# Two heads' maxima in the two halves of TensorE's rows, and a dense result loaded into the key buffer

## The chip, the cores and the metric

The kernel runs on one core of one Trainium2 chip. The metric is the device time of one execution in microseconds (us). Lower is better. Engines are named as in the profile: PE is TensorE, PEld its weight loads, DVE VectorE, ACT ScalarE, POOL GpSimd, SP SyncE, whose queue (SPq) issues all the DMAs of this kernel.

## The reference

The input `x` has 2048 rows of 512 numbers. Two branches are computed from it and mixed by a gate, one number per row:

```python
g = sigmoid((x * gate_w).sum(-1))
a = attention(x, wqkv) @ wo      # 32 heads of 16; a query sees itself and the 255 keys before it
b = gelu(x @ w1 + b1) @ w2 + b2  # 1792 hidden units, tanh form of GELU
out = g * a + (1 - g) * b
```

All of it is float32. In attention, `scores = q @ k * 16**-0.5`, masked to the sliding window, softmax over the keys, times `v`.

## The kernel before, in words

**Precision.** TensorE multiplies in a rounded format (`fp32r`). To keep float32 accuracy an operand is split into a high part and the rest, and a dense product is three matmuls: high x high, high x low, low x high (`mm3`, lines 89 to 92). For attention the same three terms are stacked along the contraction: a head's 16 numbers take 32 rows with high and low interleaved, and 16 rows more for the third term.

**The stacks.** `qs` and `ks` (lines 168 and 169) hold the stacked queries and keys of four heads at a time: two pairs `pr`, and in each pair two heads `s`. Rows 0 to 31 are the first head's high and low parts, rows 32 to 63 the second head's, rows 64 to 79 and 80 to 95 their third terms. Rows 96 to 103 of `qs` take the negated maxima of the rows, and `ks` has ones there at the head's own columns (`own`, `clear_k`). In `ks` each head's keys stand in columns of their own, blocks of 64 alternating between the heads, and the other head's rows are zero in them, so that a product over all rows gives one head's scores. `load_k` and `att_load` (lines 348 to 373) fill them by DMA from the stores SK and SQ, one chunk of 512 columns at a time.

**Attention** runs in 8 groups of four heads, each with 16 blocks of 128 queries: 128 units. For a unit:

- `att_max` (line 385): for each of four heads one matmul of the 128 queries with up to 384 keys into a PSUM buffer `sm` (three of them), and then on VectorE a reduction with the mask that gives the row's maximum (L399). `att_rows` negates and transposes four blocks' maxima, and GpSimd puts them into rows 96 to 103 of `qs`.
- `att_exp` (line 425): eight units later, four matmuls of keys with queries (L435, all 128 rows, so the maxima are subtracted in the product) into buffers `st`, ScalarE's exponential, and GpSimd's masks.
- `att_pv` (line 456): every fourth unit, the products with the values, in tiles of 64 rows by 32 columns (L476), into one buffer `st` and one `sm`. The result goes to memory (ND), is normalised in `att_norm`, and is stored as OT.

**The dense branch** is a generator (`dense`, line 726): the projections for q, k and v, then eight turns of `mlp` (four stretches of 512 rows, each with two halves of the hidden units; `gelu` is spread over ACT and DVE), then `final`, which multiplies the attention result with `wo` and mixes. A turn of the first half stores its sum in YA, a turn of the second half adds it and stores YB. `load_y` (line 676) loads YB into weight buffers `w`: the first stretch in the last turn, the others in `final`. `scale_y` multiplies with 1 - g in place, and L716 adds it to g times the product.

**The order** is written out by hand. The main loop (line 755) goes through the units; for each of four steps it issues one maximum (`i ^ XOR`), one score, and lets the generator run until 574 ns of dense matmuls are issued (`fill`, a quarter of STEP). What the other engines do is put into a list with a due time (`after`); `tick` advances a clock by an assumed cost of each matmul and issues what is due; `need` forces what must be there. So the assumed costs and delays (GELU, LAND, YLAND) set the order of instructions on ACT, DVE, POOL and SP, and not their time.

Of the kernel before, what the change touches and what calls it, by code (L numbers as in the profile page):

```python
# [9 lines left out]
F32 = mybir.dt.float32  # L10
# [8 lines left out]
T = 512  # L19
# [13 lines left out]
def gated_mix(ctx: ExitStack, tc: tile.TileContext, x, wqkv, wo, w1, b1, w2, b2, gate_w, out):  # L33
# [11 lines left out]
    def f32(ap):  # L45
        return ap.bitcast(F32)
# [3 lines left out]


    SQ = [dr.tile([H, 16, 2, T], F32, name=f"SQ{t}") for t in range(NT)]
    SK = dr.tile([H, 16, 2, S], F32, name="SK")
    SV = [dr.tile([T, H, 17], F32, name=f"SV{t}") for t in range(NT)]
    XT = [dr.tile([NC, 128, 2, T], F32, name=f"XT{t}") for t in range(NT)]
# [22 lines left out]
    for k in (0, 1):  # L78
        nc.gpsimd.affine_select(out=own[96:104], in_=own[96:104], pattern=[[-2, 4]], compare_op=ALU.not_equal,
                                fill=1.0, base=-k, channel_multiplier=1)  # L80
    nms = cp.tile([128, RB, 32], F32R, name="nm")
    nc.gpsimd.memset(f32(nms), 0.0)
    vbuf = cp.tile([128, 2, NB * 68 + 16], F32, name="vbuf")
# [76 lines left out]
    def load_now(key):  # L160
        load_raw(key)
        after(LAND, split, key, nc.vector)

# [182 lines left out]
    def load_k(g_, c, prs):  # L348


        need(("qk", c, NC + g_ // 2))
        for pr in range(prs.start, prs.stop):
            for s in range(2):
                src = SK[4 * g_ + 2 * pr + s]
                for r, n, part in ((32 * s, 32, src.rearrange("d u c -> (d u) c")), (64 + 16 * s, 16, src[:, 0])):
                    v = f32(ks[r:r + n, pr])
                    k0, m = (c * T, NB) if s == 0 else (c * T - 64, NB) if c else (64, NB - 1)
                    to = v[:, 2 * k0 + 64:2 * k0 + 64 + 256 * m] if s else v[:, 2 * k0:2 * k0 + 256 * m]
                    to = to.rearrange("r (n x) -> r n x", x=256)
                    to = to[:, :, 0:128] if s else to[:, :, 64:192]  # L360
                    nc.sync.dma_start(to, part[:, k0:k0 + 128 * m].rearrange("r (n x) -> r n x", x=128))
                    if s and c == 0:
                        nc.sync.dma_start(v[:, 0:64], part[:, 0:64])
                    if s and c == NT - 1:
                        nc.sync.dma_start(v[:, 2 * S - 64:2 * S], part[:, S - 64:S])

    def att_load(g_, c, q_only=False):
        need(("qk", c, g_ // 2))
        if not q_only:
            load_k(g_, c, slice(0, 2))  # L370
        src, to = SQ[c][4 * g_:4 * g_ + 4], f32(qs[:, :, c * T:(c + 1) * T])
        nc.sync.dma_start(to[0:64], src.rearrange("(a s) d u c -> (s d u) a c", a=2))
        nc.sync.dma_start(to[64:96], src[:, :, 1].rearrange("(a s) d c -> (s d) a c", a=2))

    def att_load_v(g_, c):
        need(*[("v", c, b) for b in range(NB)])
# [8 lines left out]
    def att_max(g_, b, i):  # L385

        if b % RB == 0 and (g_, b // RB) not in Ms:
            Ms[g_, b // RB] = sb.tile([128, RB, 4], F32, tag="M", bufs=2, name=f"M{g_}_{b}")
        M = Ms[g_, b // RB]
        k0 = max(b - 2, 0) * 128  # L390
        w = (b + 1) * 128 - k0
        pr, s = divmod(i, 2)
        p = ps.tile([128, 384], F32, tag="sm", bufs=3, name=f"sm{g_}_{b}_{i}")
        nc.tensor.matmul(p[:, :w], qs[0:96, pr, b * 128:(b + 1) * 128], of_head(ks[0:96, pr, 2 * k0:2 * (k0 + w)], s),  # L394
                         start=True, stop=True)
        junk = sb.tile([128, 384], BF16, tag="jm", bufs=1, name=f"jm{g_}_{b}_{i}")

        def red():
            nc.vector.tensor_tensor_reduce(junk[:, :w], p[:, :w], mask[:, 384 - w:384], 1.0, -3e38,  # L399
                                           ALU.add, ALU.max, M[:, b % RB, i:i + 1])  # L400
            done.add(("max", g_, b, i))
        tick(w / 2.4 + 13)
        after(100, red)

    def att_rows(g_, rb):
# [198 lines left out]
    def ya_load(k):  # L604
# [7 lines left out]
        else:  # L612
            need(("y", 0, t, b))
            nc.sync.dma_start(ya, YA[t][slice(b * 128, (b + 1) * 128)])

    def mlp(n):
        half, t = TURNS[n]
        if n == 0:
            ya_load(0), ya_load(1)
        last = n % NT == NT - 1  # L620
        xt = xts[t]
        hs = []
        for i in range(HF):
            f = half * HF + i
            need(("w", ("w1", f)))
            w = wt["w1", f]
            p = ps.tile([128, T], F32, tag="d", bufs=2, name=f"u{t}_{f}")
            for c in range(NC):
                mm3(p, w[:, 0, c], w[:, 1, c], xt[:, c, 0], xt[:, c, 1], c == 0, c == NC - 1)
                yield MM3  # L630
            h = sb.tile([128, 2, T], F32R, tag="h", bufs=8, name=f"h{t}_{f}")
            after(100, gelu, p, f, h)
            hs.append(h)
            if last and later:
                load(later.pop(0))
        if n == 0:
            for c in range(NC):
                nc.sync.dma_start(XT[t][c], f32(xt[:, c]))
        if n + 1 < len(TURNS) and TURNS[n + 1][1] != t:
            load_x(TURNS[n + 1][1], f"mx{half}")  # L640
        ps_ = {}

        def y_start(b):
            if n + 1 == len(TURNS) and b == 2:
                load_o(0)
            if n + 1 == len(TURNS) and b == 3:
                load_y(0)
            ps_[b] = ps.tile([128, D], F32, tag="d", bufs=2, name=f"y{t}_{half}{b}")

        def y_end(b):  # L650
            ts = slice(b * 128, (b + 1) * 128)
            y = sb.tile([128, D], F32, tag="sq", bufs=2, name=f"yo{t}_{half}{b}")
            nc.vector.scalar_tensor_tensor(y, ps_[b], 0.5, yas.pop(n * NB + b), op0=ALU.mult, op1=ALU.add)
            ya_load(n * NB + b + 2)
            nc.sync.dma_start((YA, YB)[half][t][ts], y)
            done.add(("y", half, t, b))


        turns = [(0, i) for i in range(HF - 1)] + [(1, i) for i in range(YSWAP)] + [(0, HF - 1)]
        turns += [(1, i) for i in range(YSWAP, HF)] + [(b, i) for b in range(2, NB) for i in range(HF)]  # L660
        for b, i in turns:
            ts = slice(b * 128, (b + 1) * 128)
            if i == 0:
                y_start(b)
            need(hs[i].name, ("w", ("w2", half * HF + i)))
            w = wt["w2", half * HF + i]
            mm3(ps_[b], hs[i][:, 0, ts], hs[i][:, 1, ts], w[:, 0], w[:, 1], i == 0, i == HF - 1)
            yield MM3
            if last and b == NB - 1 and later:
                load(later.pop(0))  # L670
            if i == HF - 1:
                after(100, y_end, b)

    ybs = {}

    def load_y(t):

        need(*[("y", 1, t, b) for b in range(NB)])
        for i in range(NB // 2):
            v = f32(sb.tile([128, 2, T], F32R, tag="w", bufs=14, name=f"yb{t}_{i}"))  # L680
            nc.sync.dma_start(v, YB[t].rearrange("(i j p) f -> i p j f", j=2, p=128)[i])
            for j in range(2):
                ybs[t * NB + 2 * i + j] = v[:, j]

    def scale_y(nb):

        nc.scalar.activation(ybs[nb], ybs[nb], AF.Copy, scale=g1[:, nb:nb + 1])
        done.add(("yb", nb))

    def final(t):  # L690
        ot = xts["o", t]
        if t < NT - 1:
            load_o(t + 1, range(NC) if t < NT - 2 else range(NC - 1))
        for i in ((1, 2), (3,), (), ())[t]:
            load_y(i)
        for b in range(NB):
            ts = slice(b * 128, (b + 1) * 128)
            nb = t * NB + b
            if t == NT - 2 and b == 2:
                load_o(t + 1, range(NC - 1, NC))  # L700
            after(YLAND if nb == 0 else 0, scale_y, nb)
            a = sb.tile([128, 2, 320], F32, tag="pt", bufs=PTS, name=f"ao{nb}")
            a = a.rearrange("p a b -> p (a b)")[:, 0:D]
            n = LASTN if nb == NT * NB - 1 else 1
            for k in range(n):
                cs = slice(k * D // n, (k + 1) * D // n)
# [6 lines left out]

                def ev(p=p, nb=nb, a=a, cs=cs):
                    need(("yb", nb))
                    nc.vector.scalar_tensor_tensor(a[:, cs], p, g[:, nb:nb + 1], ybs[nb][:, cs],  # L716
                                                   op0=ALU.mult, op1=ALU.add)
                    nc.sync.dma_start(out[nb * 128:(nb + 1) * 128, cs], a[:, cs])
                after(100, ev)
# [35 lines left out]
    for u in range(-LEAD, NU):  # L755
# [3 lines left out]
        for i in range(4):  # L759
            for op in ORDER:  # L760
                if op == "s" and u >= 0:
                    att_exp(u // NKB, u % NKB, i)
                if op == "m" and m < NU:
                    att_max(gm, bm, i ^ XOR)
                if op == "p" and i == PVAT and u >= 1:
                    att_pvs(u - 1)
                if op == "f":
# [4 lines left out]
            att_load(*chunks.pop(0))  # L772
        if u % NB == 0 and u >= 0:
            att_load_v(*divmod(u // NB, NT))
    att_pvs(NU - 1)
    for c in run:
        tick(c or 0)
# [4 lines left out]
MM3 = 3 * 227  # L782
LPOS = 0
LASTN = 2
YLAND = 3200
WARM = (7, 3)
RB = 4
NKB = S // 128
# [3 lines left out]
START = 117e3  # L792
NORM = 4500
YSWAP = 3
GELU = (700, 1500, 3600, 4600, 6000, 7000)
XAT = 3
ORDER = 'mspf'
XOR = 1
PACE = 4000.0
LAND = 10500.0  # L800
LANDO = 5000.0
# [24 lines left out]
```

## Time and profile before

| | us |
|---|---|
| median of 3 runs | 776.58 (775.4 to 778.53) |
| profiled execution | 779.54 |
| its span | 777.6 |
| PE busy | 751.4 |
| DVE busy | 533.4 |
| ACT busy | 432.8 |
| POOL busy | 384.9 |

The granted TensorE clock was 0.993 over the span. The page gives the busy time of each engine and the chain of work that ended last; a view of groups gives, for each line and engine, the number of instructions, their busy time, the mean of one, and what the engine waited for before them. Views by window cut out a stage. Matmuls are pipelined: their records overlap, and the end of a record is modelled, so what one costs is read from the distance of two starts.

### The profile page before, as it was taken

How to read it: one execution, taken by the hardware profiler on the slowest of the kernel's cores; microseconds unless marked ns; L12 is line 12 of the kernel's file. 1: busy time of each engine (PE TensorE's matmuls, PEld its weight loads, DVE VectorE, ACT ScalarE, POOL GpSimd, SP SyncE). 2: the span in 40 equal slices, each digit the busy share in tenths (PEclk: the TensorE clock that was granted, in tenths of full speed). 3: DMA queues.
4: the chain of work that ended last, by engine and by line, in shares of the span. 5: the costliest groups of instructions: out<-in, count | busy, mean ns of one | idle time of the engine just before them, and what ended most of it. 6: DMA issues, size and time to landing. Idle time of an engine off the chain costs nothing.

```text
span 777.6 us, 18427 instructions
## 1 busy us (share of the span) xinstructions
PE 751.4 (97%) x6102; PEld 626.0 (81%) x6102; DVE 533.4 (69%) x1548; ACT 432.8 (56%) x945; POOL 384.9 (50%) x1125
## 2 busy tenths in 40 slices
PE   8999999989999999999999999999999999999978
PEld 5888888867888888788878877888888788878757
DVE  4532323889679868876997798679778867974433
ACT  4434433367468547754874676458548744875341
POOL 2200000028666765775676677657756774786000
PEclk9999999999999999999999999999999999999989
DMA  9986857755643665674436756642765563355772
GB/s 284 368 299 199 312 194 223 238 186 174 172 105 80 205 186 135 179 196 121 101 108 189 193 141 208 192 114 66 214 190 151 161 180 103 87 160 172 261 246 107
DMA packets 137680, 139.91 MB, mean 180 GB/s; under 512 B 53360, under 2 KB 88688, under 8 KB 137584
## 3 DMA queue, kind: packets, MB, share of 16 engines
q1 hardware_dynamic: 137584, 138.73, 59.8%
q8 instruction: 48, 0.79, 0.4%
q14 instruction: 48, 0.39, 0.2%
HBM read 83.63 MB, written 55.05 MB: 178 GB/s over the span
## 4 chain that ended last, share of the span: by engine, by line
PE 81%; DVE 8%; DMA 4%; issue 3%; ACT 2%; SPq 1%; DVEq 0%; ACTq 0%
PE sm L394 10%; PE st L435 8%; PE y L90 7%; PE y L91 6%; PE y L92 6%; PE u L90 5%; PE u L91 5%; PE u L92 5%; PE pv_st L476 4%; PE qk L92 4%; PE qk L90 4%; PE qk L91 4%; DVE jm L399 4%; PE pv_sm L476 4%; PE v L92 2%
## 5 line engine op out<-in xcount | busy, mean ns | idle before, releaser
L399 DVE CUSTOM_DVE_ANT_0 jm<-sm,mask 128x384 bf16<-128x384 f32 (+2 forms) x512 | 269.7, 527 | 67.7 <-PE sm L394 39.2
L450 ACT ACTIVATE pt<-st 128x320 f32<-128x320 f32 (+4 forms) x512 | 206.1, 421 | 134.1 <-PE st L435 127.1
L441 POOL TENSOR_SCALAR_AFFINE_SELECT pt<-pt 64x128 f32<-64x128 f32 x512 | 175.7, 343 | 187.4 <-ACT pt L450 167.5
L394 PE MATMUL sm<-ks,qs 96*128 96x384 f32 (+2 forms) x512 | 172.0, 339 | 10.2 <-DVE M L399 8.3
L435 PE MATMUL st<-qs,ks 128*128 128x320 f32 (+4 forms) x512 | 155.5, 306 | 0.7 <-ACT pt L450 0.7
L444 POOL TENSOR_SCALAR_AFFINE_SELECT pt<-pt 64x128 f32<-64x128 f32 x448 | 155.4, 347 | 0.0
L394 PEld LDWEIGHTS sm<-ks,qs 96*128 96x128 f32 x512 | 96.5, 188 | 43.1 <-DVE M L399 20.3
L435 PEld LDWEIGHTS st<-qs,ks 128*128 128x128 f32 x512 | 97.6, 191 | 18.2 <-ACT pt L450 1.1
L90 PE MATMUL y<-w,h 128*128 128x512 f32 x224 | 90.2, 403 | 0.0
L91 PE MATMUL y<-w,h 128*128 128x512 f32 x224 | 88.4, 395 | 0.0
L92 PE MATMUL y<-w,h 128*128 128x512 f32 x224 | 87.6, 391 | 0.0
L419 POOL CAST qs<-tt 8x256 fp32r<-8x256 f32 x128 | 61.5, 481 | 47.0 <-PE u L92 38.6
L90 PE MATMUL u<-mx,w 128*128 128x512 f32 x196 | 80.4, 410 | 0.0
L91 PE MATMUL u<-mx,w 128*128 128x512 f32 x196 | 77.3, 394 | 0.0
L92 PE MATMUL u<-mx,w 128*128 128x512 f32 x196 | 76.8, 392 | 0.0
L476 PE MATMUL pv_st<-pt,vbuf 64*32 64x320 f32 (+4 forms) x1408 | 73.5, 347 | 0.0
L476 PE MATMUL pv_sm<-pt,vbuf 64*32 64x320 f32 (+4 forms) x1408 | 73.0, 346 | 0.0
L476 PEld LDWEIGHTS pv_st<-pt,vbuf 64*32 64x32 f32 x1408 | 56.4, 106 | 4.7
L476 PEld LDWEIGHTS pv_sm<-pt,vbuf 64*32 64x32 f32 x1408 | 53.9, 106 | 7.5 <-issue 2.1
L251 DVE TENSOR_TENSOR qke<-qk,qke 128x512 fp32r<-128x512 f32 x32 | 22.1, 690 | 48.9 <-ACT qke L248 38.4
L248 ACT ACTIVATE qke<-qk 128x512 fp32r<-128x512 f32 x32 | 19.1, 598 | 55.8 <-PE qk L92 36.9
L92 PEld LDWEIGHTS y<-w,h 128*128 128x128 f32 x224 | 42.1, 188 | 9.8
(123 smaller groups left out, 1316.7 us busy)
## 6 DMA issues: line engine op xcount, KB each, us to landing
mx<-XT SPq DMA_DIRECT2D x24, 512.0 KB
SQ<-qke SPq DMA_DIRECT2D x16, 512.0 KB
SK<-qke SPq DMA_DIRECT2D x16, 512.0 KB
qs<-SQ SPq DMA_DIRECT2D x32, 256.0 KB
ND<-nd SPq DMA_DIRECT2D x32, 256.0 KB
ks<-SK SPq DMA_DIRECT2D x112, 64.0 KB
raw_w<-in_B_w_dram SPq DMA_DIRECT2D x28, 256.0 KB
SV<-vx SPq DMA_DIRECT2D x16, 272.0 KB
```

The source lines that it names most:

```text
L90: nc.tensor.matmul(p, lh, rh, start=first, stop=False)
L91: nc.tensor.matmul(p, lh, rl, start=False, stop=False)
L92: nc.tensor.matmul(p, ll, rh, start=False, stop=last)
L251: nc.vector.tensor_sub(e[:, 1 - h], p, f32(e[:, h]))
L394: nc.tensor.matmul(p[:, :w], qs[0:96, pr, b * 128:(b + 1) * 128], of_head(ks[0:96, pr, 2 * k0:2 * (k0 + w)], s), start=True, stop=True)
L399: nc.vector.tensor_tensor_reduce(junk[:, :w], p[:, :w], mask[:, 384 - w:384], 1.0, -3e38, ALU.add, ALU.max, M[:, b % RB, i:i + 1])
L419: nc.gpsimd.tensor_copy(dst, tt[32 * i:32 * i + 8].unsqueeze(1).broadcast_to([8, 2, RB, 32]))
L435: nc.tensor.matmul(p[:, :w], ks[:, pr, 2 * k0:2 * k0 + 128], qs[:, pr, k0:k0 + w], start=True, stop=True)
L441: nc.gpsimd.affine_select(out=v[:, :, 0:64], in_=v[:, :, 0:64], pattern=[[0, 2], [1, 64]], compare_op=ALU.is_ge, fill=0.0, base=0, channel ...
L444: nc.gpsimd.affine_select(out=v[:, :, W:W + 64], in_=v[:, :, W:W + 64], pattern=[[0, 2], [-1, 64]], compare_op=ALU.is_ge, fill=0.0, base=- ...
L450: nc.scalar.activation(pt[:, pr, :w], p[:, :w], AF.Exp, scale=SCALE)
L476: nc.tensor.matmul(pv[r // 64][32 * i:32 * i + 32, q - c * T:e - c * T], vs(i, r), rhs(r), start=start, stop=last, skip_group_check=True, ...
```

## The change

1. **Row layout.** The first head's rows of a pair are 0 to 31 and 40 to 55, the second head's 64 to 95 and 104 to 119. The maxima's rows 96 to 103 now lie among the second head's, so each load of a chunk of queries first writes zeros there, from a small store ZQ. The queries' load is four DMAs in place of two, and the zeros are a fifth.
2. **The maxima's products.** Each contracts 56 rows of one half of the array, at tile position (0, 0) or (64, 0). The two heads of a pair are issued one right behind the other: two pairs in a unit, at the first and the third step. The planner's clock counts half the cost for each.
3. **The dense result.** The last turn keeps its four blocks on chip: two in a weight buffer, two in the `sq` buffers. The other three stretches are loaded during the last group of heads, into the columns of `ks` whose keys are no longer read. `scale_y` writes into the output buffer instead of in place, and the delay YLAND is gone.
4. **Delays.** GELU's due times are shorter.

```diff
+    ZQ = dr.tile([8, 2, T], F32, name="ZQ")
...
+    zero = sb.tile([128, 2, T], F32, tag="h", bufs=8, name="zero")
+    nc.gpsimd.memset(zero[0:8], 0.0)
+    nc.sync.dma_start(ZQ, zero[0:8])
...
-                for r, n, part in ((32 * s, 32, src.rearrange("d u c -> (d u) c")), (64 + 16 * s, 16, src[:, 0])):
+                for r, n, part in ((64 * s, 32, src.rearrange("d u c -> (d u) c")), (64 * s + 40, 16, src[:, 0])):
...
-        nc.sync.dma_start(to[0:64], src.rearrange("(a s) d u c -> (s d u) a c", a=2))
-        nc.sync.dma_start(to[64:96], src[:, :, 1].rearrange("(a s) d c -> (s d) a c", a=2))
+        nc.sync.dma_start(to[96:104], ZQ)
+        for s in range(2):
+            r = 64 * s
+            nc.sync.dma_start(to[r:r + 32], src.rearrange("(a s) d u c -> s (d u) a c", s=2)[s])
+            nc.sync.dma_start(to[r + 40:r + 56], src[:, :, 1].rearrange("(a s) d c -> s d a c", s=2)[s])
...
-        nc.tensor.matmul(p[:, :w], qs[0:96, pr, b * 128:(b + 1) * 128], of_head(ks[0:96, pr, 2 * k0:2 * (k0 + w)], s),
-                         start=True, stop=True)
+        rows = slice(64 * s, 64 * s + 56)
+        nc.tensor.matmul(p[:, :w], qs[rows, pr, b * 128:(b + 1) * 128], of_head(ks[rows, pr, 2 * k0:2 * (k0 + w)], s),
+                         start=True, stop=True, tile_position=(64 * s, 0))
...
-        tick(w / 2.4 + 13)
+        tick((w / 2.4 + 13) / 2)
...
-            if n + 1 == len(TURNS) and b == 3:
-                load_y(0)
...
-            y = sb.tile([128, D], F32, tag="sq", bufs=2, name=f"yo{t}_{half}{b}")
+            if n + 1 < len(TURNS) or b >= 2:
+                y = sb.tile([128, D], F32, tag="sq", bufs=2, name=f"yo{t}_{half}{b}")
+            else:
+                if b == 0:
+                    ybs["w"] = sb.tile([128, 2, T], F32, tag="w", bufs=14, name="yo")
+                y = ybs["w"][:, b]
...
-            nc.sync.dma_start((YA, YB)[half][t][ts], y)
+            if n + 1 < len(TURNS):
+                nc.sync.dma_start((YA, YB)[half][t][ts], y)
+            else:
+                ybs[t * NB + b] = y
...
-            v = f32(sb.tile([128, 2, T], F32R, tag="w", bufs=14, name=f"yb{t}_{i}"))
+            v = f32(ks[:, i, 2 * t * T:2 * (t + 1) * T]).rearrange("p (j f) -> p j f", j=2)
...
-        nc.scalar.activation(ybs[nb], ybs[nb], AF.Copy, scale=g1[:, nb:nb + 1])
+        nc.scalar.activation(a, ybs[nb], AF.Copy, scale=g1[:, nb:nb + 1])
...
-        for i in ((1, 2), (3,), (), ())[t]:
-            load_y(i)
...
-            after(YLAND if nb == 0 else 0, scale_y, nb)
+            after(0, scale_y, nb, a)
...
-                    nc.vector.scalar_tensor_tensor(a[:, cs], p, g[:, nb:nb + 1], ybs[nb][:, cs],
+                    nc.vector.scalar_tensor_tensor(a[:, cs], p, g[:, nb:nb + 1], a[:, cs],
...
-                if op == "m" and m < NU:
-                    att_max(gm, bm, i ^ XOR)
+                if op == "m" and m < NU and i % 2 == 0:
+                    att_max(gm, bm, i), att_max(gm, bm, i + 1)
...
+        if u >= NU - NKB + NB and u % NB == 1:
+            load_y((u % NKB) // NB - 1)
...
-GELU = (700, 1500, 3600, 4600, 6000, 7000)
+GELU = (650, 1400, 3300, 4200, 5400, 6400)
```

More of the change, by code (lines that the diff above doesn't have):

```diff
@@ L614, in ya_load @@
             nc.sync.dma_start(ya, YA[t][slice(b * 128, (b + 1) * 128)])
+    ybs = {}
     def mlp(n):
@@ L672, in mlp @@
                 after(100, y_end, b)
-    ybs = {}
     def load_y(t):
@@ L683, in load_y, with scale_y @@
                 ybs[t * NB + 2 * i + j] = v[:, j]
-    def scale_y(nb):
-        nc.scalar.activation(ybs[nb], ybs[nb], AF.Copy, scale=g1[:, nb:nb + 1])
+    def scale_y(nb, a):
+        nc.scalar.activation(a, ybs[nb], AF.Copy, scale=g1[:, nb:nb + 1])
         done.add(("yb", nb))
@@ L784 @@
 LASTN = 2
-YLAND = 3200
 WARM = (7, 3)
@@ L794 @@
 YSWAP = 3
-GELU = (700, 1500, 3600, 4600, 6000, 7000)
+GELU = (650, 1400, 3300, 4200, 5400, 6400)
 XAT = 3
 ORDER = 'mspf'
-XOR = 1
 PACE = 4000.0
```

## The prediction

> **What bounds the kernel now.** I read the page first, then the windows of the attention stage and of the end, then the timelines of TensorE (PE) and of its weight loads (PEld), then who waits for whom, and last the queue of SyncE (SPq).
>
> ```profile
> span 777.6 us, 18427 instructions
> PE 751.4 (97%) x6102; PEld 626.0 (81%) x6102; DVE 533.4 (69%) x1548; ACT 432.8 (56%) x945; POOL 384.9 (50%) x1125
> ...
> PE 81%; DVE 8%; DMA 4%; issue 3%; ACT 2%; SPq 1%; DVEq 0%; ACTq 0%
> ```
>
> TensorE is busy for 97% of the span, and 81% of the chain that ended last is its own work. Two windows tell how near the next engine is, and what the end looks like (busy us of PE, PEld, DVE, ACT, POOL; granted clock, DMA share, GB/s).
>
> ```profile
> 160.00:700.00 540.00, 527.89 (x4917) 443.00 (x4916) 433.45 (x1336) 341.55 (x763) 359.20 (x1044) 1.00 0.55 154
> 720.00:778.00 58.00, 46.92 (x204) 38.27 (x202) 21.84 (x33) 17.33 (x29) 0.00 (x0) 0.94 0.61 202
> ```
>
> While attention runs beside the dense branch (160 to 700), TensorE has 528 of 540 us and VectorE 433 (80%). In the last 58 us TensorE lacks 11 us. So what the change does to TensorE's time per unit of attention is paid one for one, until VectorE is met.
>
> **The products of the maxima as they are.** The change touches the 512 matmuls of L394 and their reductions on L399. In the steady state they stand like this (start, duration).
>
> ```profile
> L399 DVE CUSTOM_DVE_ANT_0 jm<-sm,mask 128x384 bf16<-128x384 f32 (+2 forms) x512 | 269.7, 527 | 67.7 <-PE sm L394 39.2
> L394 PE MATMUL sm<-ks,qs 96*128 96x384 f32 (+2 forms) x512 | 172.0, 339 | 10.2 <-DVE M L399 8.3
> ```
>
> ```profile
> 404.67 0.40 PE L92 MATMUL y<-w,h 128*128 128x512 f32 x1
> 404.91 0.34 PE L394 MATMUL sm<-ks,qs 96*128 96x384 f32 x1
> 405.08 0.31 PE L435 MATMUL st<-qs,ks 128*128 128x320 f32 x1
> 405.23 0.40 PE L90 MATMUL y<-w,h 128*128 128x512 f32 x1
> ```
>
> The durations overlap, so the price of an instruction is the distance of two starts: 0.23 us for a dense matmul of 512 columns, 0.17 for a maximum of 384, 0.15 for a score of 320. The weights of the next matmul come in behind the running one and cost nothing. A maximum has 96 rows, yet it follows and precedes matmuls of 128 rows at these full-rate distances: it does not change how the array is divided.
>
> **Two halves do run side by side.** The products with the values (L476) use 64 rows each; `pv_st` and `pv_sm` name the two halves.
>
> ```profile
> 413.55 0.43 PE L476 MATMUL pv_sm<-pt,vbuf 64*32 64x320 f32 x1
> 413.56 0.43 PE L476 MATMUL pv_st<-pt,vbuf 64*32 64x320 f32 x1
> ...
> 413.82 0.43 PE L476 MATMUL pv_sm<-pt,vbuf 64*32 64x320 f32 x1
> ```
>
> The halves start 0.01 us apart, and the next round starts 0.27 later. So I take a pair of maxima to last 0.17 + 0.01 in place of 2 x 0.17. That is the gain: 0.16 us for each of 256 pairs, 224 of them 384 columns wide; 16 of 256 columns and 16 of 128 save, by width, about 0.11 and 0.05. Sum: 224 x 0.16 + 16 x 0.16 = 38 us at most.
>
> **What dividing the array costs.** These are the rows where TensorE goes from undivided matmuls to L476 and back, each with its weight loads.
>
> ```profile
> 412.57 0.36 PE L435 MATMUL st<-qs,ks 128*128 128x320 f32 x1
> 412.86 0.24 PE L476 MATMUL pv_sm<-pt,vbuf 64*32 64x64 f32 x1
> ...
> 415.04 0.22 PE L476 MATMUL pv_sm<-pt,vbuf 64*32 64x64 f32 x1
> 415.21 0.50 PE L90 MATMUL y<-w,h 128*128 128x512 f32 x1
> 415.54 0.40 PE L91 MATMUL y<-w,h 128*128 128x512 f32 x1
> ```
>
> ```profile
> 412.51 0.19 PEld L435 LDWEIGHTS st<-qs,ks 128*128 128x128 f32 x1
> 412.85 0.10 PEld L476 LDWEIGHTS pv_sm<-pt,vbuf 64*32 64x32 f32 x1 [0.15 <-issue]
> ...
> 415.20 0.19 PEld L90 LDWEIGHTS y<-w,h 128*128 128x128 f32 x1
> ```
>
> On the way in, the score ends at 412.93 by its record, and the first divided weights are not loaded before 412.85: not during the score, as between undivided matmuls, but 0.08 before its end. No wait is recorded ("issue"). On the way out the same: the last divided product ends at 415.26, L90's weights start at 415.20, 0.06 before it. And these weights are no longer hidden: L90 lasts 0.50 instead of 0.40, and L91 follows after 0.33 instead of 0.23. So a change of the division lets the array run empty, and then shows a weight load of 128 columns (0.10 us).
>
> The kernel has 32 such visits now. In the changed one every pair is two products on 64 rows of the array (tile positions (0,0) and (64,0)), and each stands between undivided matmuls: 256 visits more, 512 changes of division. In: after a dense matmul, whose record lasts 0.40, the pair's weights would start at 0.40 - 0.08 = 0.32 and count for 0.10, so the pair streams at 0.42 instead of 0.24: +0.18 us. Out: the pair's record would last 0.34, the next weights start at 0.34 - 0.06 = 0.28 and show for 0.10, so the score streams 0.38 after it instead of 0.17: +0.21. Against the 0.16 saved, a wide pair costs 0.39 - 0.16 = +0.23 us; 224 x 0.23 = 51.5. The narrow ones: 16 x (0.39 - 0.11) + 16 x (0.39 - 0.05) = 10. Sum: **+61 us**. The weak step is that the rows show it for tiles of 64 rows by 32 columns, and the new ones are 64 by 128. Bounds: -38 (no emptying) and +61 + 256 x 0.11 = +89 (the two halves' weights also come one after the other). I take +61, since the nearest rows, with the same division of the rows, show it at each visit.
>
> The Trainium skill ("TensorEngine Tiling (Array Packing)", Tiling Modes, Key Properties) says that a change of the tiling mode drains TensorE, and lists 64x128 as a mode beside 128x128. The trace agrees for 64x32 (weights at 0.08 and 0.06 us before a record's end); for 64x128 no row here shows it.
>
> **Waits of the maxima.** What L394 waited for now (us, times):
>
> ```profile
>   DVE M L399: 28.6, 55
>   DVE nd L498: 5.4, 11
> ```
>
> This adds TensorE's and the weight loads' idle time, some of it twice; the excess in the distances is about 20 us. Three buffers hold the products. A pair takes two at once, so its second waits for the reduction of the pair before, about 2 us earlier, where a maximum now waits for the third before it, 3 us earlier. That costs; but with TensorE at 12% more per unit VectorE falls further below its 80%. I take -5, between -20 and +8.
>
> **Loads.** A chunk's queries were two issues; now there are five, with the zeros.
>
> ```profile
> 415.20 0.62 SPq L372 DMA_DIRECT2D qs<-SQ  x1
> 415.86 0.59 SPq L373 DMA_DIRECT2D qs<-SQ  x1
> ```
>
> Three more of 0.6 us for 32 chunks are 58 us of SyncE's time, ahead of the value loads and the stores queued behind. The cover: a chunk is loaded four units, some 17 us, before its first maximum. The zeros wait, as the queries do, for the last score that reads those columns, which stands just before the load in the order. The keys move to other rows in as many issues. Cost nothing; without the cover 1.8 us a chunk. The one memset of zeros and its store at the start are under 1 us. The shorter planner time and the GELU delays only shift orders on ACT and DVE by a place; 0, between -4 and +4.
>
> **The end.** The loads of the dense branch's result, and how the end goes now:
>
> ```profile
> 716.41 1.43 SPq L681 DMA_DIRECT2D yb<-YB  x3
> 719.85 7.26 SPq L561 DMA_DIRECT2D or<-OT  x4
> ```
>
> ```profile
> 718.27 8.43 DMA OT<-num
> ```
>
> ```profile
> 743.28 0.39 PE L92 MATMUL a<-wo,ot 128*128 128x512 f32 x1
> 749.36 0.76 PE L90 MATMUL a<-wo,ot 128*128 128x512 f32 x1 [5.69 <-DVE ao L716]
> 749.92 0.63 PE L91 MATMUL a<-wo,ot 128*128 128x512 f32 x1
> ```
>
> Three loads of 512 KB are issued just ahead of a store that lands only after 8.43 us; SyncE stands 7.26 us for it, and everything behind it is late. TensorE stops for 5.69 us and comes back with matmuls 0.43 apart instead of 0.23, thirteen of them: 2.6 us. The change issues six of the eight loads during the last group of heads, into columns of `ks` that are no longer read, and leaves out the last two with their four stores. So the 8.3 us may go, or half, if the chain of normalising, storing and reloading is late by itself. What is late next is that chain's own landings. I take -6, between -9 and +2 (the earlier loads lie beside value loads).
>
> **Sum.** +61 - 5 - 6 = +50. The profiled execution took 779.5 us (span 777.6), the median of the runs is 776.6, 3 lower; the edits count alike in both. Forecast: 776.6 + 50 = **827 us**, by its own bounds (entries 0.05 cheaper each way, or the end unchanged and VectorE's waits at +8) 800 to 848.
>
> **The rivals.**
> 1. *No emptying: faster.* If 64 by 128 can follow 128 by 128 as 96 rows follow 128 now, the pair's weights are hidden and the gain of 38 us stands. Then VectorE is met: 433 us in 540 - 38 = 502 is 86%, with two products thrown at it at once; I add 8 (0 to 20) of waits. -38 + 8 - 6 = -36: 741 us (730 to 757). For it: halves beside each other in L476. Against it: each visit of L476 starts by emptying. It decides from a cost per visit below 0.16 us. The skill's page "TensorE: Matmul & The Clock Gate" (Part 3) gives a packed group one matmul's time plus about 4 ns for each tile, and names no price for entering; by that alone this rival would hold.
> 2. *Emptying, but the weights are loaded meanwhile.* 61 - 512 x 0.10 = +10, less 11: 776 us, no change. Against it: the 0.50 of L90.
> 3. *The change doesn't do what it says:* the two products run one after the other, with no emptying. The maxima cost what they do, the end gives -6, the pairs' waits +2: 773. Against it: 0.01 us between the halves.
> 4. *Emptying, and the halves' weights one after the other:* +28 on the forecast: 855.
>
> **How the numbers follow.** Forecast 0.58, rival 1 0.22, rival 2 0.07, rival 3 0.06, rival 4 0.07. A measurement of this kernel tells about 0.5% from no change, 773 to 780. Faster by more: rival 1, and half of 2 and 3: 0.28. Within: the other half, 0.06. Slower: 0.66. The range of 8 in 10 must reach into rival 1: from 742 (half of it below, 0.11) to 848 (most of rival 4 and a tail above, 0.08).
>
> **What would show it.** In the profile after: the distance from the dense matmul to the pair's first streaming and from the pair to the score. By the forecast each pair's weight loads start only near the end of the matmul before it, the score behind it has a record of 0.41 instead of 0.31, and attention ends some 55 us later. By rival 1 the pair's weights start during the matmul before, its two starts are 0.01 apart, and the score follows 0.17 later. In the end, the 5.69 us stop should be gone. The forecast is wrong if the array needn't run empty between 128 and 64 rows.

## The result and the profile after

The changed kernel takes **829.28 us** (median of 4 runs, 827.53 to 837.98), the kernel before 777.56: a ratio of **1.0686 (95% interval 1.0634 to 1.0738)**. The forecast was 827. The profiled execution took 828.17 us for a span of 826.3, 48.7 more than before. These are the rows of its page: the span, the engines, and the chain.

```profile
span 826.3 us, 18557 instructions
PE 806.6 (98%) x6102; PEld 577.7 (70%) x6102; DVE 540.8 (65%) x1548; ACT 432.9 (52%) x945; POOL 379.3 (46%) x1126
...
PE 88%; DVE 5%; DMA 2%; issue 2%; ACT 1%; SPq 1%; POOL 0%; DVEq 0%; ACTq 0%
```

TensorE's share of the chain rose from 81 to 88%, and VectorE's fell from 8 to 5. The weight loads are busy for 48 us less, though there are as many: two halves load at once. The windows of the attention stage and of the end (same columns as before):

```profile
160.00:746.00 586.00, 576.98 (x4902) 394.53 (x4901) 441.43 (x1339) 338.58 (x757) 347.69 (x1030) 0.99 0.51 143
764.00:826.30 62.30, 54.02 (x325) 44.42 (x323) 25.86 (x40) 21.86 (x41) 4.29 (x11) 0.95 0.52 170
```

Where the 48.7 us lie: from the first to the last score (L435 before, L444 after) 552.0 us became 601.7, **+49.7**; from the last product with the values to the end 58.1 became 55.6, **-2.5**; the first score comes 1.6 later. Now the maxima themselves, as timeline of TensorE and of its weight loads (x2 is a pair):

```profile
435.92 0.39 PE L96 MATMUL y<-w,h 128*128 128x512 f32 x1
436.24 0.44 PE L403 MATMUL sm<-ks,qs 56*128 56x384 f32 x2
436.61 0.42 PE L444 MATMUL st<-qs,ks 128*128 128x320 f32 x1
436.87 0.40 PE L94 MATMUL y<-w,h 128*128 128x512 f32 x1
```

```profile
435.69 0.19 PEld L96 LDWEIGHTS y<-w,h 128*128 128x128 f32 x1
436.24 0.19 PEld L403 LDWEIGHTS sm<-ks,qs 56*128 56x128 f32 x2 [0.36 <-DVE M L408]
436.61 0.19 PEld L444 LDWEIGHTS st<-qs,ks 128*128 128x128 f32 x1 [0.19 <-issue]
436.72 0.19 PEld L94 LDWEIGHTS y<-w,h 128*128 128x128 f32 x1
```

This is the picture that the forecast drew. The dense matmul ends by its record at 436.31, and the pair's weights start at 436.24, 0.07 before that. The two products run side by side, and each record lasts 0.44 instead of 0.34, which is the weight load that nothing hides. The pair ends at 436.68, the score's weights start at 436.61, again 0.07 before; the score's record is 0.42 instead of 0.31, and the next dense matmul follows it after 0.26 instead of 0.15. "DVE M" in the brackets is the releaser that came last by the records; the same gap of 0.07 us before the end of a record stands where no wait is recorded ("issue").

What the maxima's products waited for in the changed kernel (us, times; idle time of TensorE and of the weight loads added):

```profile
  issue: 44.1, 121
  DVE M L408: 41.1, 102
  DMA qs<-SQ: 4.8, 4
```

Before it was 28.6 us in 55 waits for VectorE; now 102 idle stretches of 0.4 us carry its name, nearly all of them the emptying. And the end, as rows of the chain, of TensorE and of SyncE's queue:

```profile
786.52 6.33 DMA OT<-num
```

```profile
792.58 0.39 PE L96 MATMUL a<-wo,ot 128*128 128x512 f32 x1
798.03 0.77 PE L94 MATMUL a<-wo,ot 128*128 128x512 f32 x1 [5.06 <-DVE ao L729]
798.59 0.63 PE L95 MATMUL a<-wo,ot 128*128 128x512 f32 x1
```

```profile
773.17 2.48 SPq L570 DMA_DIRECT2D or<-OT  x2
```

SyncE's first stand of 7.26 us, behind the second of the last four stores of OT, is down to 2.48, as forecast. But TensorE's stop is still there: 5.06 us for 5.69. It now hangs on the third of these stores, the one of 6.33 us. That one held SyncE up in the kernel before too:

```profile
737.96 6.69 SPq L561 DMA_DIRECT2D or<-OT  x3
```

The slow matmuls behind the stop are there as well, 0.43 us apart: the granted clock is 0.50 from 797.5 to 804, and in the kernel before it was 0.50 from 748.6 to 755.

### The profile page after: what moved, and what is told of

It reads as the page before. It is cut to its first block, busy times and chain, and to the rows that moved or that the text cites. A ratio compares the mean times of both kernels' runs of the same rounds, so it can differ in the third digit from the quotient of the medians.

```text
span 826.3 us, 18557 instructions
## 1 busy us (share of the span) xinstructions
PE 806.6 (98%) x6102; PEld 577.7 (70%) x6102; DVE 540.8 (65%) x1548; ACT 432.9 (52%) x945; POOL 379.3 (46%) x1126
## 4 chain that ended last, share of the span: by engine, by line
PE 88%; DVE 5%; DMA 2%; issue 2%; ACT 1%; SPq 1%; POOL 0%; DVEq 0%; ACTq 0%
PE st L444 13%; PE sm L403 11%; PE y L94 6%; PE y L95 6%; PE y L96 6%; PE u L94 6%; PE u L96 5%; PE u L95 5%; PE pv_st L485 4%; PE qk L94 4%; PE qk L96 4%; PE qk L95 4%; PE pv_sm L485 3%; DVE jm L408 2%; PE v L96 2%; PE v L94 2%
## 5 line engine op out<-in xcount | busy, mean ns | idle before, releaser
L459 ACT ACTIVATE pt<-st 128x320 f32<-128x320 f32 (+4 forms) x512 | 210.0, 422 | 194.1 <-PE st L444 188.6
L450 POOL TENSOR_SCALAR_AFFINE_SELECT pt<-pt 64x128 f32<-64x128 f32 x512 | 181.4, 354 | 241.8 <-ACT pt L459 223.9
L444 PE MATMUL st<-qs,ks 128*128 128x320 f32 (+4 forms) x512 | 174.5, 353 | 0.3 <-ACT pt L459 0.3
L453 POOL TENSOR_SCALAR_AFFINE_SELECT pt<-pt 64x128 f32<-64x128 f32 x448 | 144.6, 323 | 0.0
L444 PEld LDWEIGHTS st<-qs,ks 128*128 128x128 f32 x512 | 93.5, 188 | 53.0 <-issue 30.4
L403 PE MATMUL sm<-ks,qs 56*128 56x384 f32 (+2 forms) x512 | 117.3, 428 | 8.5 <-DMA qs<-SQ 4.8
L403 PEld LDWEIGHTS sm<-ks,qs 56*128 56x128 f32 x512 | 51.9, 183 | 101.6 <-issue 44.1
L256 DVE TENSOR_TENSOR qke<-qk,qke 128x512 fp32r<-128x512 f32 x32 | 22.1, 691 | 48.7 <-ACT qke L253 38.7
```

Source lines behind the costliest of these rows:

```text
L256: nc.vector.tensor_sub(e[:, 1 - h], p, f32(e[:, h]))
L403: nc.tensor.matmul(p[:, :w], qs[rows, pr, b * 128:(b + 1) * 128], of_head(ks[rows, pr, 2 * k0:2 * (k0 + w)], s), start=True, stop=True, ti ...
L444: nc.tensor.matmul(p[:, :w], ks[:, pr, 2 * k0:2 * k0 + 128], qs[:, pr, k0:k0 + w], start=True, stop=True)
L450: nc.gpsimd.affine_select(out=v[:, :, 0:64], in_=v[:, :, 0:64], pattern=[[0, 2], [1, 64]], compare_op=ALU.is_ge, fill=0.0, base=0, channel ...
L453: nc.gpsimd.affine_select(out=v[:, :, W:W + 64], in_=v[:, :, W:W + 64], pattern=[[0, 2], [-1, 64]], compare_op=ALU.is_ge, fill=0.0, base=- ...
L459: nc.scalar.activation(pt[:, pr, :w], p[:, :w], AF.Exp, scale=SCALE)
```

## The experiments

**Theory:** between the undivided array and tiles of 64 by 128 TensorE runs empty and shows a weight load, each way; a visit (into the divided array and out again) costs 0.39 us, whatever is done in it. **Rivals:** the pairing in three buffers, the five loads for a chunk, the moved loads or the planner's clock cost the time; or the cost hangs on each half-row product.

### e1_undivided: the division taken back

```diff
-        rows = slice(64 * s, 64 * s + 56)
+        rows = slice(0, 120)
...
-                         start=True, stop=True, tile_position=(64 * s, 0))
+                         start=True, stop=True)
```

> The changed kernel with one thing taken back: the maxima's products contract rows 0 to 119 undivided (the other head's rows of the keys are zero), at no tile position. Row layout, zeros, pairs one behind the other, the result's loads and the delays stay. Theory (each change of the array's division lets it run empty and shows a weight load): the distances around a maximum go back to 0.23 and 0.17 us, 256 visits go away, and the time falls from 829 to 772 to 782. Rival (the pairing in three buffers, the five loads or the moved loads cost the time): it stays above 815.

Measured: 801.33 us, ratio 1.0309 (1.0288 to 1.033). Between the two: 28 us come back, not 50. On TensorE all is as the theory has it (the pair's second product starts 0.17 after the first, no weight load shows):

```profile
406.33 0.39 PE L96 MATMUL u<-mx,w 128*128 128x512 f32 x1
406.56 0.51 PE L403 MATMUL sm<-ks,qs 120*128 120x384 f32 x2
406.90 0.31 PE L444 MATMUL st<-qs,ks 128*128 128x320 f32 x1
407.06 0.39 PE L94 MATMUL u<-mx,w 128*128 128x512 f32 x1
```

So other parts of the change cost some 24 us once the division is gone, which my step for them (nothing for the loads and the delays, -5 for the waits) had missed. The next kernels price them. The trace shows only some 18 of the 24: it is of an execution of 795.62 us with a granted clock of 0.994, while the other four took 800 to 802 us at 0.987 to 0.989.

### e2_pairs: the pairing alone

```diff
-                if op == "m" and m < NU:
-                    att_max(gm, bm, i ^ XOR)
+                if op == "m" and m < NU and i % 2 == 0:
+                    att_max(gm, bm, i), att_max(gm, bm, i + 1)
```

> The kernel before, with the two maxima of a pair of heads issued one right behind the other, undivided, twice in a unit instead of one in each step. Theory: only the waits for the three buffers change; ratio to before 0.995 to 1.015. Rival (the pairing is what costs): 1.04 or more.

Measured: 788.96, ratio 1.0146 (1.0128 to 1.0164), the upper end of what was expected: **11 us for pairing alone**. The products' idle time in this kernel:

```profile
  DVE M L399: 58.1, 84
```

58.1 us of waits for the reductions in place of 28.6 (TensorE's and the weight loads' added, so the time lost is less than the difference). That is the wait for a third buffer that the prediction named.

### e3_dense: the moved loads of the dense result alone

The third part of the change (see the diff above) on the kernel before.

> The kernel before with only the third part of the change: the dense result loaded during the last group into the columns of the keys, the last turn's blocks kept on chip. By the forecast's step for the end, 6 us less: 771, ratio 0.992. By the profile of the changed kernel, in which TensorE's stop of 5 us near the end is still there and the end as a whole is some 2.5 us shorter: 774, ratio 0.997. Rival (the moved loads collide with the value loads of the last group): 778 or more, ratio above 1.001.

Measured: 774.14, ratio **0.9943 (0.9923 to 0.9964)**, faster than both kernels; 3.7 us less by the medians, of the 6 of the forecast. SyncE's stand behind the second store of OT, its chain and its waits:

```profile
720.00 3.76 SPq L561 DMA_DIRECT2D or<-OT  x2
```

```profile
733.97 6.09 DMA OT<-num
```

```profile
PE a L90 <- DVE ao L720: 3.1, 1, 3.1
```

With no load of the dense result near it, the second store holds SyncE up for 3.76 us instead of 7.26, so that part of the forecast's step stands. TensorE's stop is 3.1 us, where it was 5.69. What is left of it hangs on the third store, which lands after 6.09 us with no such load near it either. So the rest of the stop belongs to the chain of normalising, storing and reloading itself; what makes the third store take so long was not tried.

### e4_singles: a visit for each maximum

```diff
-                if op == "m" and m < NU and i % 2 == 0:
-                    att_max(gm, bm, i), att_max(gm, bm, i + 1)
+                if op == "m" and m < NU:
+                    att_max(gm, bm, i)
```

> The changed kernel with one maximum in each step, as before: each product on 64 rows has a visit of its own, 512 visits in place of 256, and nothing runs beside it. Theory (a price of about 0.39 us for each visit, the product's own 0.17 on top): 256 x (0.39 + 0.17) = 143 us more than the changed kernel, some 970, or down to 950 as VectorE's waits go. Rival (the price is paid for each product on half the rows, whatever stands beside it): about 830.

Measured: 946.78 (one run), 3 below the lower end of what was expected and 117 above the changed kernel. The rival by product is out, and the rows show the visits' price. A visit with one product:

```profile
415.99 0.39 PE L96 MATMUL y<-w,h 128*128 128x512 f32 x1
416.31 0.44 PE L403 MATMUL sm<-ks,qs 56*128 56x384 f32 x1
416.68 0.42 PE L444 MATMUL st<-qs,ks 128*128 128x320 f32 x1
416.94 0.39 PE L94 MATMUL y<-w,h 128*128 128x512 f32 x1
```

From dense matmul to dense matmul this takes 0.95 us, and so does the pair of the changed kernel (435.92 to 436.87): the second product is free. Undivided, one maximum takes 405.23 - 404.67 = 0.56: 0.39 for a visit. And the groups of heads (from first score to first score) now take 91.6 to 91.8 us each from the second to the seventh, and TensorE is never idle in them. With 64 visits x 0.39 = 25 off, TensorE would need 66.7 us for a group with no wait at all; this is an estimate. Before, a group took 67.4 to 72.1 (69.8 in the mean of the first seven): some 3 us of each, 25 in all by this estimate, were waits, most of them recorded as waits for VectorE. The changed kernel still has some (74.6 to 82.3 us for each of the first seven groups, where 66.7 + 32 x 0.22 = 73.7 would do). A slower TensorE covers them, which would explain most of the step from the 143 us expected to 117.

### e5_clock and e6_div_clock: the planner's clock and GELU's delays back

```diff
-        tick((w / 2.4 + 13) / 2)
+        tick(w / 2.4 + 13)
...
-GELU = (650, 1400, 3300, 4200, 5400, 6400)
+GELU = (700, 1500, 3600, 4600, 6000, 7000)
```

> The undivided variant of the changed kernel (801 us) with the planner's clock and GELU's delays as they were before: the full cost of a maximum in the clock, GELU at 700 to 7000. What is left of the change is the row layout with its five loads, the pairs, and the moved loads. The kernel before with pairs alone took 789, and the moved loads alone gave -3.4. Theory (a clock that counts half for the maxima issues the weights' loads too early for their buffers, and SyncE stands before them with the keys and queries behind): 783 to 789, and the first group of heads takes 72 us, not 80. Rival (the five loads a chunk and the zeros cost the time): about 801, the first group stays at 80.

> The changed kernel, divided as it is, with the planner's clock and GELU's delays as they were before. Theory of the clock: some 8 us less than 829, since only the first group's stop goes: 819 to 824. Rival (loads): 827 to 831.

Measured: undivided 792.12, ratio 1.0177 (1.0147 to 1.0207), 9 less than e1 and 3 more than expected at most; divided 827.82, ratio 1.0635 (1.0605 to 1.0664), in the rival's range, and no difference from the changed kernel that can be told. In the undivided one the first group of heads falls from 80.4 to 72.5 us. A row of SyncE's queue in e1, the same load in e5, and the wait that followed in e1:

```profile
174.59 5.09 SPq L141 DMA_DIRECT2D raw_w<-in_B_w_dram  x2
```

```profile
176.34 0.36 SPq L141 DMA_DIRECT2D raw_w<-in_B_w_dram  x1
```

```profile
PE sm L403 <- DMA qs<-SQ: 5.7, 1, 5.7
```

In e1 SyncE stands 5.09 us before a weight load whose buffer isn't free, and keys and queries stand behind it: the next queries go out at 203.79, in e5 at 198.51. A maximum then waits 5.7 us for its queries, a wait that e5 doesn't have. The traces explain only part of the 9 us: the two profiled executions are 3.5 us apart (794.0 and 790.5), because later groups take back some of what the first one gains, and the rest goes with the granted clock, 0.987 to 0.989 in the other executions of e1 and 0.994 to 0.998 in those of e5. Both settings were put back together, so whether the clock or GELU's delays matter is not shown. In the divided kernel the expected 5 to 10 us are not there: its first group still falls, 82.3 to 77.1, but other groups take that back.

### e7_fours: both pairs in one visit

```diff
-                if op == "m" and m < NU and i % 2 == 0:
-                    att_max(gm, bm, i), att_max(gm, bm, i + 1)
+                if op == "m" and m < NU and i == 0:
+                    for j in range(4):
+                        att_max(gm, bm, j)
...
-        p = ps.tile([128, 384], F32, tag="sm", bufs=3, name=f"sm{g_}_{b}_{i}")
+        p = ps.tile([128, 384], F32, tag=("sm", "st")[i // 3], bufs=3, name=f"sm{g_}_{b}_{i}")
```

> The changed kernel with both pairs of a unit in one visit, at the first step: 128 visits instead of 256, the fourth product in a score's PSUM buffer. Theory (0.39 us for a visit, nothing for a product beside another): 128 x 0.39 = 50 us less, 779, and up to 800 if four reductions at once make the next products and the scores wait. Rival (the cost hangs on the products, not on the visits): 825 to 832.

Measured: 827.3, ratio 1.0623 (1.0598 to 1.0648). By the time alone the rival would win. The profile tells them apart. A visit that waits for nothing, and one that waits:

```profile
432.65 0.39 PE L96 MATMUL y<-w,h 128*128 128x512 f32 x1
432.97 0.61 PE L403 MATMUL sm<-ks,qs 56*128 56x384 f32 x4
433.51 0.41 PE L444 MATMUL st<-qs,ks 128*128 128x320 f32 x1
433.76 0.40 PE L94 MATMUL y<-w,h 128*128 128x512 f32 x1
```

```profile
403.17 0.44 PE L403 MATMUL sm<-ks,qs 56*128 56x384 f32 x2
404.64 0.44 PE L403 MATMUL sm<-ks,qs 56*128 56x384 f32 x2 [1.03 <-DVE nd L507]
405.01 0.56 PE L444 MATMUL st<-qs,ks 128*128 128x320 f32 x2
```

Four products take 1.11 us from dense to dense, two more than a pair's 0.95 by only 0.16: the price is the visit's. But in other visits the second pair finds no buffer. The fourth product also takes one of the scores' three buffers, and the idle time before the scores (TensorE's and the weight loads' added) for ScalarE's exponential goes from 2.6 us in the changed kernel to this:

```profile
  ACT pt L459: 39.4, 71
```

In the window of the attention stage:

```profile
160.00:746.00 586.00, 547.93 (x4858) 393.04 (x4866) 445.45 (x1333) 336.39 (x754) 343.25 (x1026) 0.98 0.51 143
```

TensorE is busy 29 us less than in the changed kernel in the same 586 us, and idle 38 instead of 9. Being idle isn't all: the record of the granted clock has it at half for 27 us of this window (seven times) and for 7 us in the changed kernel, so part of the busy time is slower work; half the difference, 10 us, is an estimate of the most that it can cost. What the visits gave, the buffers took, and the clock with them. That these half-rate stretches come from the stops is not shown.

### e8_layout: the row layout and its five loads

The kernel e5, with one undivided maximum in each step as before (`att_max(gm, bm, i ^ 1)`).

> The kernel before with the moved loads of the dense result, the new row layout and its five loads a chunk, but one undivided maximum in each step as before, and the planner's clock as before. Beside the kernel with the moved loads alone (774, ratio 0.994) it prices the layout and its loads. Theory from the variant with pairs (792, where pairs alone and the moved loads explain 789 - 3): the loads cost 3 to 7 us, 777 to 781. Rival (loads are hidden, the rest came from the pairs meeting the moved loads): 773 to 775.

Measured: 783.53, ratio 1.0065 (1.0046 to 1.0085), against 774.14 (0.9943) without layout and loads: **9 us**, more than expected, where the prediction had put nothing. The trace is of its longest execution, 788.59 us. Two of its waits:

```profile
PE sm L403 <- DMA qs<-SQ: 2.4, 1, 2.4
PEld sm L403 <- issue: 3.2, 2, 2.8
```

A maximum waits 2.4 us for its queries, so SyncE's cover does give out; two longer stops (2.1 us at a maximum, 1.2 us at the values) carry VectorE's name. Which of the five loads, the zeros or the split queries, costs most was not tried.

## Why the prediction was right, point by point

1. **Emptying and a shown weight load at tiles of 64 by 128:** right, and it decides. A wide pair takes 0.95 us from dense to dense; undivided it takes 407.06 - 406.33 = 0.73 (e1). So +0.22 for a pair, where the forecast had +0.23, and some 256 x 0.22 = 56 us for all pairs, where it had 61. The cost of entering and leaving is what made rival 1 fail. The Trainium skill ("TensorEngine Tiling (Array Packing)", Tiling Modes) says that a change of mode drains TensorE; the trace now agrees for 64x128 (weights 0.07 us before the record's end, both ways). The Trainium skill ("TensorE: Matmul & The Clock Gate", Part 3) gives about 4 ns between packed tiles; the trace agrees, with the starts inside a pair 0.003 us apart.
2. **Waits, -5:** the balance is about right (+49.7 in the attention stage, of which the 240 pairs inside it make 240 x 0.22 = 53), and so is its reason, that pairs cost waits and a slower TensorE covers them. What it lacked is the size. Each part alone adds waits: pairs 11 us, the clock with GELU's delays 9, and in the divided kernel they are covered. From e5 to e6, where only the division differs, the attention stage grows by 30 us (571.4 to 601.0) and not by 53: some 23 us are waits that a slower TensorE takes over.
3. **Loads, 0:** wrong for the undivided kernel (9 us), and hidden beside the division, as far as the sum tells. The four-unit cover was argued from the distance of issue and use, and not from what else stands in SyncE's queue. In the changed kernel four waits for queries, 4.8 us in all, are left of it.
4. **The end, -6:** half right. Alone -3.7 us (e3), in the changed kernel -2.5. The second store was held up by the loads beside it, or by the last stores of YB that went with them: SyncE's stand behind it fell from 7.26 to 3.76 (e3) and 2.48 us. The stop "should be gone" and is 5.06 us. The step that failed is the one that laid most of the stop to this store. The chain's own landings, which the forecast had named as what is late next, keep most of it: the third store was late before (6.69 us of SyncE's time), and without any such load beside it still takes 6.09 to 6.33. The 2.6 us of slow matmuls, which the forecast counted as part of the stop, are a granted clock of 0.50.
5. **The sum:** +50 forecast, 51.7 measured. That it comes so close is in part luck. In a ladder of medians from the kernel before (777.9), the moved loads (774.1), the layout (783.5), the pairs (792.1), the clock and delays (801.3) and the division (829.3) add -4, +9, +9, +9 and +28 us. So by time the division, put in last, costs half of what its visits take by the rows; the other half was spent before on waits that it covers. The forecast had the one large term right, and was spared the three of 9 us, because beside the division they cost together nearly nothing (56 - 4 is already 52). It had argued this cover for the pairs, and not for the loads and the clock. Two of its bounds don't come out of their terms: with the end unchanged and the waits at +8 the upper one is 846 and not 848, and rival 1 with 20 us of waits and the end at -6 is 753 and not 757.

## What to carry to other kernels

A gain by concurrent tiles is paid for at the door: count the changes of the array's division, in and out, and price each from a place where the trace already has one; here a visit of 0.39 us carried 0.17 us of saved work. When a part of a change makes the busiest engine slower, the waits of others can vanish beside it, so parts measured alone don't add up: price the ladder step by step, from the variant that will be kept. The part worth keeping here is the moved load of the dense result (0.9943).

## What the runs showed that was not expected

The planner's assumed costs set no times, and yet the halved cost in its clock, together with GELU's shorter delays, cost 9 us in the undivided kernel. The place that the trace shows is a stand of SyncE before a buffer that isn't free, with unrelated loads behind it (5.09 us, where the same load took 0.36 with both put back). And pairing two products with no other edit cost 11 us, with VectorE at 80%: the distance of two uses of a buffer matters before an engine is full.
